# A fused window-attention and two-MLP kernel: w3's product over all eight PSUM banks, and the later pairs' right factors made ahead and kept in DRAM

## The chip, the cores and the metric

The kernel runs on one core of a Trainium2 chip. The metric is device microseconds for one execution. Five engines work side by side, each through its own instructions in their order: PE (matrix products; PEld is its weight load), DVE (VectorE), ACT (ScalarE), POOL (GpSimd) and SP, which here only issues transfers. PE writes its products to PSUM, which has eight banks; the other operands lie in SBUF.

## The reference, cut to what matters

The input is 4 x 576 = 2304 tokens. A causal attention with a window of 128 and a linear bias per head gives x (2304 x 512). Then two MLPs follow:

```python
h = x @ w_in                       # 512 -> 2048
g = s * np.maximum(h, 0.0) ** 2 + b
x2 = g @ w_out                     # 2048 -> 512
a, c = x2 @ w1, x2 @ w2            # 512 -> 1024 each
out = ((a * c) @ w3) @ w_out2      # 1024 -> 1024 -> 512
```

The weights come as 64-bit floats and are turned into 32-bit floats on the chip. The products need more than one pass of PE's fp32r format, so an operand is kept as a high and a low part (hi = the rounded value, lo = value - hi), and each product is three passes: hi·hi, hi·lo, lo·hi.

## The kernel before, in words

Tokens are worked in six tiles of 384. An attention task for a head and a tile runs beside the first MLP of an earlier tile. The changed lines lie in what comes after and around the last tile:

- **The last MLP tile** (`slot`, `mlp_h`, `mlp_relu`, `mlp_g`, `mlp_gl`, `mlp_x`). For each of 16 chunks of d_ff, PE makes `hp` (12 matmuls, L488), ACT and DVE make `gh` and `gl` of it (the high and low part), and PE adds 12 matmuls into the four `acc` banks (L537). The attention is over by then, and each slot offers four places to put other work in. There `w_tick` decodes w1 and w2 chunk by chunk (`w_chunk`: two loads `wr<-w`, an ACT pass, three DVE passes per matrix that join the 64-bit halves, then sums s1 to s4 on DVE, then four splits into hi on ACT and lo on POOL by `split_to`), and `late_load` brings back the prepared pieces of w3 and w_out2.
- **w3's product** (`w3_unit`): w3 @ w_out2 is made once, as w3o, 192 matmuls of 512 columns, in two groups of four PSUM banks; each group is copied out and split (ACT L579, DVE L580) when its eight units are done.
- **The three pairs.** Two token tiles make a pair. x2 @ w1 and x2 @ w2 are taken by blocks with seven products instead of eight (Strassen's scheme): left factors A11 ... S4 come from `w_chunk`, right factors B11, B21, T1, T2, T4, B22, T3 from `x_steps`, each for k = 0, 1, so 14 tiles of a hi and a lo part. `pair_chunk` runs 42 matmuls for each of eight chunks (L736), DVE and POOL combine them into p (DVE L822 for the first tile of the pair, POOL L828 for the second), `p_split` makes ph and pl (ACT L753, DVE L758), and `out_mm` takes p to the output, nine matmuls (L772): for the first tile of the pair inside the loop, one chunk late, for the second tile after the loop (`out_mm(2q+1, c)`, with `out_mm(2q, 7)` among them).
- **Between pairs**: the right factors of pair 0 are made beside w3's product. Those of pairs 1 and 2 are made after the loop of the pair before, beside its last nine `out_mm`: loads of x2 from DRAM (`x2_load`), sums on DVE (L702), the hi parts on ACT (L594), the lo parts on POOL (L595).

Inside these the order on each engine is set by a scheduler that plays the program through a timeline, so what stands in the program is only where work may go. Matmuls of the pairs are kept in program order. SP issues all transfers, in one queue. Tiles of one tag share a few buffers, and a new one waits until an old one is free: `t` (6 buffers: x2 loads and the products' copies m4, m5), `z` (2), `gh` and `gl` (2 each), `w` (33).

Of the kernel before, what the change touches and what calls it, by code (L numbers as in the profile page):

```python
# [18 lines left out]
DM = H * D  # L19
# [16 lines left out]
PASSES = ((0, 0), (0, 1), (1, 0))  # L36


@with_exitstack
def kernel(  # L40
# [481 lines left out]
    def mlp_x(t, c):  # L522
# [5 lines left out]
        for m in range(KD):  # L528
            ms = slice(m * P, (m + 1) * P)
            if t == 0:  # L530
                nc.tensor.matmul(  # L531
                    out=x2acc[m], lhsT=wo[c][:, ms], rhs=g,
                    start=(c == 0), stop=(c == NC1 - 1),
                )
                continue
            for n, (l, r) in enumerate(PASSES):
                nc.tensor.matmul(  # L537
                    out=x2acc[m], lhsT=wo[c][:, l, ms], rhs=g[r],
                    start=(c == 0 and n == 0), stop=(c == NC1 - 1 and n == 2),
                )  # L540
# [25 lines left out]
    def w3_unit(ig, j, accs):  # L566
        if j == 0:
            pool, tag = ((ps_rot, "rot"), (ps_acc, "acc"))[ig]
            accs[:] = [pool.tile([P, DM], F32, tag=tag, name="w3a") for _ in range(4)]
        for i in range(4):  # L570
            for n, (l, r) in enumerate(PASSES):
                nc.tensor.matmul(  # L572
                    out=accs[i], lhsT=w3g[ig, j][:, l, i * P:(i + 1) * P], rhs=wo2s[j][:, r, :],
                    start=(j == 0 and n == 0), stop=(j == NC2 - 1 and n == 2),
                )
        if j == NC2 - 1:
            for i in range(4):
# [18 lines left out]

    def w_chunk(c):
# [48 lines left out]
        tt(out=s3, in0=a11, in1=a21, op=ALU.subtract)  # L646
        yield 1 - c % 2
# [4 lines left out]
        split_to((d[:, 0, dc], d[:, 1, dc]), a22, nc.gpsimd)  # L652
# [3 lines left out]
        for names, src in ((("A11", "A12"), z1), (("S1", "S2"), sv[:, :DM]), (("S3", "S4"), sv[:, DM:])):  # L656
# [5 lines left out]
            split_to((t[:, 0, :], t[:, 1, :]), src, nc.gpsimd)  # L662
# [16 lines left out]
    def x2_load(q, k):  # L679
        for nm, t, m in (  # L680
            ("11", 2 * q, k), ("21", 2 * q, 2 + k), ("12", 2 * q + 1, k), ("22", 2 * q + 1, 2 + k)
        ):
# [64 lines left out]
    def p_split(src):  # L747
        ph = gp.tile([P, TT], F32R, tag="gh", name="ph")
        pl = gp.tile([P, TT], F32R, tag="gl", name="pl")
# [48 lines left out]
    def pair_chunk(q, c):  # L798
# [8 lines left out]
        tt(out=m1, in0=d, in1=m1, op=ALU.add)  # L807
        e = ps_rot.tile([P, TT], F32, tag="rot", name="d5")
# [304 lines left out]
```

## Time and profile before

| | us |
|---|---|
| median of 3 runs (906.1 to 927.08) | 907.81 |
| the profiled execution | 908.04 |
| its span | 906.3 |
| PE busy in the span, 4676 matmuls | 865.2 (95%) |
| PEld, DVE, ACT, POOL busy | 778.3, 578.5, 484.4, 419.8 |

The profile is of one execution. A row of a timeline gives start, duration, engine, line, operation and the tiles (out<-in); in brackets stands the idle time ahead of it and what ended it. Runs of like instructions are merged into one row, and xN is their count. The ends of matmuls are modelled, so PE's pace is read from the starts of rows.

### The profile page before, as it was taken

To read this page: it belongs to the slowest core of one execution; us is meant where nothing else is said; L and a number is where in the kernel's file an instruction comes from. 1 tells how busy PE (TensorE), PEld (TensorE's weight loads), DVE (VectorE), ACT (ScalarE), POOL (GpSimd) and SP (SyncE) were. 2 spreads that over 40 slices of the span, in tenths; PEclk is the share of its full clock that TensorE was granted. 3 is DMA by queue.
4 is the path that set the end of the run, shared out by engine and by line. 5 is a ranking of instruction groups with operands and counts; after the bars stand their busy time and mean duration, and the time that the engine had idled before them with its cause. 6 is when DMAs were issued, how large, how long until landed. Compare 5 with 4: busy or idle time off the path is not lost.

```text
span 906.3 us, 13449 instructions
## 1 busy us (share of the span) xinstructions
PE 865.2 (95%) x4676; PEld 778.3 (86%) x4676; DVE 578.5 (64%) x1146; ACT 484.4 (53%) x1140; POOL 419.8 (46%) x440
## 2 busy tenths in 40 slices
PE   8999898999999999999999899979997999899988
PEld 5766566999999999999999799869995999679986
DVE  5888897767888888788747952493336332553332
ACT  5766657877877777776655553342224222332222
POOL 0157657778667776677545423451116111441110
PEclk8999999999999999999999999989999999999999
DMA  8954522121444454554317576120102000110001
GB/s 312 328 199 148 188 76 88 53 76 54 138 164 167 146 192 149 181 176 159 116 71 273 186 255 238 44 73 1 35 1 70 35 8 28 62 42 1 1 1 71
DMA packets 37076, 104.38 MB, mean 115 GB/s; under 512 B 4368, under 2 KB 10512, under 8 KB 37008
## 3 DMA queue, kind: packets, MB, share of 16 engines
q1 hardware_dynamic: 37008, 103.52, 33.3%
q8 instruction: 37, 0.61, 0.3%
q14 instruction: 31, 0.25, 0.1%
HBM read 82.00 MB, written 21.50 MB: 114 GB/s over the span
## 4 chain that ended last, share of the span: by engine, by line
PE 69%; DVE 13%; issue 7%; ACT 4%; DMA 4%; POOL 2%; SPq 0%; DVEq 0%; POOLq 0%; ACTq 0%
PE acc L537 14%; PE hp L488 13%; PE d L736 10%; PE oacc L772 8%; PE u L736 7%; PE w3a L572 3%; PE pv L418 3%; PE hp L479 2%; PE acc L531 2%; DMA wr<-w 2%; PE s L296 1%; PE s L297 1%; DVE z L629 1%; DVE z L101 1%; DVE x2r L702 1%
## 5 line engine op out<-in xcount | busy, mean ns | idle before, releaser
L488 PE MATMUL hp<-x,w 128*128 128x384 f32 x960 | 186.7, 339 | 2.5 <-DVE pp L378 2.5
L537 PE MATMUL acc<-gh,w 128*128 128x384 f32 x640 | 177.3, 339 | 2.2 <-ACT gh L509 2.2
L488 PEld LDWEIGHTS hp<-x,w 128*128 128x128 f32 x960 | 167.5, 188 | 3.1 <-DVE pp L378 2.6
L828 POOL TENSOR_TENSOR p<-mc 128x384 f32<-128x384 f32 (+2 forms) x30 | 30.8, 1035 | 194.5 <-DVE mc L823 194.5
L537 PEld LDWEIGHTS acc<-gh,w 128*128 128x128 f32 x640 | 115.0, 188 | 3.6 <-ACT gh L509 3.4
L537 PE MATMUL acc<-gl,w 128*128 128x384 f32 x320 | 109.3, 342 | 4.6 <-DVE gl L517 4.5
L736 PE MATMUL d<-xb,wblk 128*128 128x384 f32 x576 | 109.1, 337 | 0.1
L736 PEld LDWEIGHTS d<-xb,wblk 128*128 128x128 f32 x576 | 102.0, 189 | 2.6 <-ACT mc L744 0.6
L346 POOL TENSOR_SCALAR pr<-pr,sm 128x128 f32<-128x128 f32 x120 | 66.1, 565 | 80.7 <-ACT z L144 24.9
L772 PE MATMUL oacc<-w3o,ph 128*128 128x512 f32 x288 | 92.1, 401 | 9.6 <-ACT ph L753 9.6
L736 PE MATMUL u<-xb,wblk 128*128 128x384 f32 x432 | 84.4, 337 | 5.9 <-ACT mc L744 5.9
L381 POOL TENSOR_SCALAR_AFFINE_SELECT pt<-pp 128x768 fp32r<-128x768 f32 x80 | 77.6, 991 | 15.4 <-PE pv L418 6.2
L819 DVE TENSOR_TENSOR mc<-d,mc 128x384 f32<-128x384 f32 x24 | 13.4, 558 | 111.4 <-PE d L736 111.4
L258 POOL TENSOR_TENSOR kb<-qkraw,ka 128x512 fp32r<-128x512 f32 x40 | 56.8, 1420 | 55.1 <-ACT ka L257 54.8
L736 PEld LDWEIGHTS u<-xb,wblk 128*128 128x128 f32 x432 | 76.4, 190 | 6.4 <-ACT mc L744 6.2
L772 PEld LDWEIGHTS oacc<-w3o,ph 128*128 128x128 f32 x288 | 54.2, 191 | 22.2 <-ACT ph L753 11.9
L517 DVE TENSOR_TENSOR gl<-r,gh 128x384 fp32r<-128x384 f32 x80 | 60.5, 757 | 19.9 <-ACT gh L509 18.9
L310 DVE CUSTOM_DVE_ANT_0 ns<-s,relm_sb 128x256 f32<-128x256 f32 (+1 forms) x144 | 52.7, 412 | 28.6 <-PE s L297 20.4
L537 PEld LDWEIGHTS acc<-gl,w 128*128 128x128 f32 x320 | 60.2, 188 | 7.3 <-DVE gl L517 7.1
L595 POOL TENSOR_TENSOR xb<-x2r,xb 128x384 fp32r<-128x384 f32 x42 | 48.1, 1175 | 38.9 <-ACT xb L594 38.9
L499 ACT ACTIVATE r<-hp 128x384 f32<-128x384 f32 x96 | 46.4, 483 | 30.6 <-PE hp L488 23.9
L772 PE MATMUL oacc<-w3o,pl 128*128 128x512 f32 x144 | 59.1, 410 | 3.1 <-DVE pl L758 2.9
(111 smaller groups left out, 1683.4 us busy)
## 6 DMA issues: line engine op xcount, KB each, us to landing
qkraw<-qk SPq DMA_DIRECT2D x41, 448.0 KB, 3.4
late<-st SPq DMA_DIRECT2D x23, 512.0 KB, 3.2
w<-late SPq DMA_DIRECT2D x23, 512.0 KB, 5.3
raw<-w_in SPq DMA_DIRECT2D x16, 512.0 KB, 5.9
raw<-w_out SPq DMA_DIRECT2D x16, 512.0 KB, 6.6
wr<-w SPq DMA_DIRECT2D x16, 512.0 KB, 3.7
st<-w3T SPq DMA_DIRECT2D x15, 512.0 KB, 3.6
vraw<-v SPq DMA_DIRECT2D x20, 256.0 KB, 2.6
```

What stands on the lines that cost most here:

```text
L258: nc.gpsimd.tensor_tensor(out=kl, in0=k_r, in1=k.bitcast(F32), op=ALU.subtract)
L310: nc.vector.tensor_tensor_reduce(out=n[:, i, cs], in0=dst[i][:, cs], in1=relm_sb[:, VARIANT.get(t * NB + i, 0), cs], scale=2.0 ** -(h + 1) ...
L346: nc.gpsimd.tensor_scalar(out=e[:, i, :], in0=e[:, i, :], scalar1=sm[:, i:i + 1], scalar2=1.0, op0=ALU.mult, op1=ALU.mult,)
L381: nc.gpsimd.affine_select(out=o[:, :, :, e, :], in_=pp.bitcast(F32), pattern=[[0, 2], [0, NB], [sign, P]], compare_op=op, fill=0.0, base=0 ...
L488: nc.tensor.matmul(out=hp, lhsT=wi[c][:, l, k * P:(k + 1) * P], rhs=xT[t, k][:, r, :], start=(n == 0), stop=(n == 3 * KD - 1),)
L499: nc.scalar.activation(out=rt[:, :TT], in_=hps.pop((t, c)), func=AF.Relu)
L517: nc.vector.tensor_tensor(out=gl, in0=rt[:, :TT], in1=gh.bitcast(F32), op=ALU.subtract)
L537: nc.tensor.matmul(out=x2acc[m], lhsT=wo[c][:, l, ms], rhs=g[r], start=(c == 0 and n == 0), stop=(c == NC1 - 1 and n == 2),)
L595: eng.tensor_tensor(out=dst[1], in0=src, in1=dst[0].bitcast(F32), op=ALU.subtract)
L736: tc.keep_in_program_order(nc.tensor.matmul(out=dst, lhsT=w[:, l, ks], rhs=xblk[bnm, k][:, r, :], start=(start and n == 0), stop=(n == 5), ...
L772: tc.keep_in_program_order(nc.tensor.matmul(out=oacc[t, i], lhsT=p[l][:, cs], rhs=w3o[c][:, r, :], start=(c == 0 and n == 0), stop=(c == N ...
L828: nc.gpsimd.tensor_tensor(out=x, in0=u2[:, n:n + w], in1=m5[:, n:n + w], op=ALU.mult)
```

## The change

- `w3_unit` takes all eight banks at once and works both groups of a unit together; the copies and splits of all eight w3o tiles stand in `w3_out`, after the product.
- The decode of w1 and w2 is offered two steps at each place of the last tile with a reserve of two buffers; the two loads of a chunk are issued inside the chunk before. Its lo parts go to DVE while the last tile runs and to POOL after it. The late pieces are loaded in the order in which the units need them, ten during the last tile and the rest beside the product.
- `x_later(q + 1)` makes the right factors of the next pair inside the chunks of pair q, a step at four places of a chunk, and stores them to DRAM; `x_fetch` brings all 14 back after the last chunk. `x_steps` is left for pair 0 alone.
- Before the last chunk of a pair, the first two splits of the second tile's p are made, one into the two `z` buffers.
- `mlp_x` makes the two passes with `gh` for all four banks first, and the pass with `gl` after them (save in the last chunk of a tile).

```diff
@@ mlp_x
+        order = [(m, n) for m in range(KD) for n in range(3)]
+        if c < NC1 - 1:
+            order.sort(key=lambda x: x[1] == 2)
+        for m, n in order if t else [(m, 0) for m in range(KD)]:
...
-            for n, (l, r) in enumerate(PASSES):
...
+            l, r = ((0, 0), (1, 0), (0, 1))[n]
...
@@ w3_unit
-    def w3_unit(ig, j, accs):
+    def w3_unit(j, accs):
         if j == 0:
-            pool, tag = ((ps_rot, "rot"), (ps_acc, "acc"))[ig]
-            accs[:] = [pool.tile([P, DM], F32, tag=tag, name="w3a") for _ in range(4)]
-        for i in range(4):
+            accs[:] = [ps_rot.tile([P, DM], F32, tag="rot", name="w3a") for _ in range(4)]
+            accs += [ps_acc.tile([P, DM], F32, tag="acc", name="w3a") for _ in range(4)]
+        for i in range(2 * 4):
...
+    def w3_out(accs):
+        for i in range(2 * 4):
+            z = wp.tile([P, 2, DM], F32R, tag="w", name="w3o")
+            nc.scalar.activation(out=z[:, 0, :], in_=accs[i], func=AF.Copy)
...
@@ w_chunk
+        if c == 0:
+            w_raws(0)
+        raws = wraw.pop(c)
...
         tt(out=s3, in0=a11, in1=a21, op=ALU.subtract)
+        if c + 1 < NC2:
+            w_raws(c + 1)
...
-            split_to((t[:, 0, :], t[:, 1, :]), src, nc.gpsimd)
+            split_to((t[:, 0, :], t[:, 1, :]), src, lo_eng[0])
@@ right factors of the later pairs
+    def x_later(q):
+        def load(nm, k):
+            r = lp.tile([P, TT], F32, tag="t", name="xs", bufs=6)
+            nc.sync.dma_start(out=r, in_=x2_at(q, nm, k))
+            return r
+        def store(nm, k, r):
+            z = zp.tile([P, TT], F32, tag="z", name="xh")
+            split_to((z.bitcast(F32R), r.bitcast(F32R)), r, nc.gpsimd)
+            d = xfd[q, nm, k]
+            nc.sync.dma_start(out=d[:, 0, :], in_=z)
+            nc.sync.dma_start(out=d[:, 1, :], in_=r)
...
+        for k in range(2):
+            for nm in ("11", "21"):
+                a = load(nm, k)
+                yield
+                store("B" + nm, k, a)
+            a, b = load("12", k), load("11", k)
+            yield
+            sub(a, a, b)
+            b = load("22", k)
+            yield
+            sub(b, b, a)
+            store("T1", k, a)
...
+    def x_fetch(q):
+        for nm in FACTORS:
+            for k in range(2):
+                y = x_tile(nm)
+                nc.sync.dma_start(
+                    out=y.rearrange("p a t -> p (a t)").bitcast(F32),
+                    in_=xfd[q, nm, k].rearrange("p a t -> p (a t)"),
+                )
+                xblk[nm, k] = y
@@ the last tile and the product
-        slot(n, n - LEAD, lambda: w_tick(3, max(0, 6 + 2 * NC2 - fresh[0] - 4 * (last + NC1 // 2 - n))))
+        slot(n, n - LEAD, lambda: w_tick(2, 2))
...
+        if n >= last + 3:
+            late_load()
+            late_load()
...
+    lo_eng[0] = nc.gpsimd
...
+    for j in range(NC2):
+        for _ in range(3):
+            if fresh[0] < 3 * NC2:
+                late_load()
+        tick(9 if fresh[0] == 3 * NC2 else 0)
+        w_tick(6, 3 if fresh[0] < 3 * NC2 else 0)
+        w3_unit(j, accs)
+        free_w[0] += 3
+        w_tick(2, 3 if fresh[0] + 2 < 3 * NC2 else 0)
+        next(prep, None)
+    w_tick(99, 8)
...
+    w3_out(accs)
+    w_tick(99)
@@ the pairs
     for q in range(NTILE // 2):
+        more = q + 1 < NTILE // 2
+        prep = x_later(q + 1) if more else iter(())
         for c in range(NC2):
...
-            if more and c == NC2 - 2:
-                x2_load(q + 1, 0)
-            pair_chunk(q, c)
+            if c == NC2 - 1:
+                assert next(prep, None) is None
+                p2 = [p_split(p2_parts(0), spare=True), p_split(p2_parts(1))]
+            pair_chunk(q, c, lambda: next(prep, None))
         if more:
-            x2_load(q + 1, 1)
-            prep = x_steps(q + 1)
-            next(prep)
+            x_fetch(q + 1)
         for c in range(NC2):
-            out_mm(2 * q + 1, c, p_split(p2_parts(c)))
-            if c == 0:
+            out_mm(2 * q + 1, c, p2.pop(0) if p2 else p_split(p2_parts(c)))
+            if c == 1:
                 out_mm(2 * q, NC2 - 1, p1s.pop())
```

How the built order moves is seen at three places. The first is DVE where w3's product ends and pair 0 begins (`wr` and `z` belong to the decode of w1 and w2, `w3a` and `w3o` to w3's product, `mc` to the products of the pair). Before:

```order
L626 TENSOR_SCALAR z<-z 128x512
L629 SCALAR_TENSOR_TENSOR z<-wr,z 128x512
L634 SCALAR_TENSOR_TENSOR z<-wr,z 128x512
L645 TENSOR_TENSOR wr<-z 128x256
L646 TENSOR_TENSOR wr<-z 128x256
L653 TENSOR_TENSOR wr<-wr,z 128x256
L654 TENSOR_TENSOR wr<-z,wr 128x256
L807 TENSOR_TENSOR mc<-d_6877,mc 128x384
L580 TENSOR_TENSOR w3o<-w3a,w3o 128x512 x4
L819 TENSOR_TENSOR mc<-d_6885,mc 128x384
L821 TENSOR_TENSOR mc<-u,mc 128x384
```

The change:

```order
L652 SCALAR_TENSOR_TENSOR z<-wr,z 128x512
L663 TENSOR_TENSOR wr<-z 128x256
L664 TENSOR_TENSOR wr<-z 128x256
L673 TENSOR_TENSOR wr<-wr,z 128x256
L674 TENSOR_TENSOR wr<-z,wr 128x256
L591 TENSOR_TENSOR w3o<-w3a,w3o 128x512 x8
L889 TENSOR_TENSOR mc<-d_6905,mc 128x384
L904 TENSOR_TENSOR mc<-d_6915,mc 128x384
L906 TENSOR_TENSOR mc<-u,mc 128x384
```

Before, the decode of the last chunks stands between the two groups of w3o, ahead of the first sums of pair 0; now the decode's end stands ahead of all eight w3o splits, and pair 0 follows them.

The second place is ACT at the end of pair 0's loop (`ph` is the hi part of p, `xb` a right factor of pair 1, `ov` an output tile). Before:

```order
L744 ACTIVATE mc<-d_7429 128x384
L753 ACTIVATE ph<-mc 128x384
L753 ACTIVATE ph<-p_6931 128x384
L594 ACTIVATE xb<-x2r 128x384 x4
L753 ACTIVATE ph<-p_6931 128x384
L594 ACTIVATE xb<-x2r 128x384
L782 ACTIVATE ov<-oacc 128x512
L753 ACTIVATE ph<-p_6931 128x256
L753 ACTIVATE ph<-p_7081 128x128
L594 ACTIVATE xb<-x2r 128x384
L753 ACTIVATE ph<-p_7081 128x384
L594 ACTIVATE xb<-x2r 128x384 x7
```

The change:

```order
L835 ACTIVATE ph<-mc 128x384
L835 ACTIVATE ph<-p_6977 128x384
L823 ACTIVATE mc<-u 128x384
L823 ACTIVATE mc<-d_7541 128x384
L823 ACTIVATE mc<-u 128x384
L823 ACTIVATE mc<-d_7567 128x384
L835 ACTIVATE ph<-mc 128x384
L835 ACTIVATE ph<-p_6977 128x256
L835 ACTIVATE ph<-p_7166 128x128
L864 ACTIVATE ov<-oacc 128x512
```

Before, the first ph of the second tile follows the last `ph<-mc`, and 13 of the 14 `xb` splits stand among the rest (the last of these rows are left off). Now a ph of the second tile stands ahead of the last chunk's copies, another one (in a `z` buffer) as far ahead as chunk 4, and no `xb` split is left there.

The third place is DVE where chunk 0 of pair 0 hands over to chunk 1. Before:

```order
L822 TENSOR_TENSOR mc<-mc 128x384
L758 TENSOR_TENSOR pl<-mc,ph 128x384
L807 TENSOR_TENSOR mc<-d_6942,mc 128x384
L819 TENSOR_TENSOR mc<-d_6950,mc 128x384
L821 TENSOR_TENSOR mc<-u,mc 128x384
```

The change:

```order
L907 TENSOR_TENSOR mc<-mc 128x384
L732 TENSOR_TENSOR xs<-xs 128x384 x2
L840 TENSOR_TENSOR pl<-mc,ph 128x384
L889 TENSOR_TENSOR mc<-d_6991,mc 128x384
L732 TENSOR_TENSOR xs<-xs 128x384
L904 TENSOR_TENSOR mc<-d_7007,mc 128x384
```

Before, the split `pl<-mc,ph` follows the product `mc<-mc` with nothing between them; now two sums for the next pair's factors (`xs`), each of which needs a load, stand ahead of it, and a third behind it.

## Rows read from the trace of the kernel before

**Rows 1.** Busy time by stretch: us, PE, PEld, DVE, ACT, POOL, granted clock, DMA share, GB/s

```profile
478.00:558.80 80.80, 74.37 (x411) 70.97 (x411) 53.43 (x78) 41.91 (x84) 27.58 (x22) 1.00 0.72 253
558.80:598.70 39.90, 39.90 (x178) 33.03 (x177) 20.78 (x27) 15.36 (x30) 21.79 (x20) 1.00 0.26 84
598.70:707.80 109.10, 97.54 (x481) 87.53 (x480) 54.12 (x85) 36.11 (x78) 35.54 (x31) 0.95 0.08 26
707.80:806.80 99.00, 94.55 (x482) 84.67 (x481) 42.06 (x70) 30.25 (x67) 26.88 (x24) 1.00 0.10 32
806.80:902.20 95.40, 92.66 (x481) 85.09 (x479) 32.76 (x63) 24.59 (x53) 10.29 (x10) 1.00 0.05 17
```

**Rows 2.** PE's waits from 500 us on: us in total, times, longest

```profile
PE oacc L772 <- ACT ph L753: 9.6, 6, 2.7
PE u L736 <- ACT mc L744: 5.9, 1, 5.9
```

**Rows 3.** The chain of waits inside pair 0: start us, us, what

```profile
618.72 2.10 PE oacc L772 x9
...
628.12 2.10 PE oacc L772 x9
```

**Rows 4.** Timeline where pair 0 begins, PE, ACT and DVE

```profile
607.86 2.29 PE L736 MATMUL u<-xb,wblk 128*128 128x384 f32 x6 [5.87 <-ACT mc L744]
...
607.34 0.47 ACT L744 ACTIVATE mc<-u 128x384 f32<-128x384 f32 x1
...
601.88 1.64 DVE L629 SCALAR_TENSOR_TENSOR z<-wr,z 128x512 uint32<-128x512 uint32 x1
...
604.16 0.42 DVE L626 TENSOR_SCALAR z<-z 128x512 uint32<-128x512 uint32 x1
604.62 0.69 DVE L629 SCALAR_TENSOR_TENSOR z<-wr,z 128x512 uint32<-128x512 uint32 x1
```

**Rows 5.** Timeline of PE from the end of pair 0's loop to pair 1

```profile
682.98 0.73 PE L772 MATMUL oacc<-w3o,ph 128*128 128x512 f32 x2 [2.62 <-ACT ph L753]
...
684.29 1.05 PE L772 MATMUL oacc<-w3o,ph 128*128 128x512 f32 x2
...
685.57 1.05 PE L772 MATMUL oacc<-w3o,ph 128*128 128x512 f32 x2
...
707.84 1.23 PE L736 MATMUL u<-xb,wblk 128*128 128x384 f32 x6
```

**Rows 6.** Timeline of one chunk's hand-over in pair 0, DVE, ACT, POOL and PEld

```profile
672.01 0.55 DVE L822 TENSOR_TENSOR mc<-mc 128x384 f32<-128x384 f32 x1
...
672.59 0.53 ACT L753 ACTIVATE ph<-mc 128x384 fp32r<-128x384 f32 x1 [0.20 <-DVE mc L822]
...
673.15 0.70 DVE L758 TENSOR_TENSOR pl<-mc,ph 128x384 fp32r<-128x384 f32 x1 [0.59 <-ACT ph L753]
673.39 1.34 POOL L595 TENSOR_TENSOR xb<-x2r,xb 128x384 fp32r<-128x384 f32 x1
...
675.20 0.19 PEld L772 LDWEIGHTS oacc<-w3o,pl 128*128 128x128 f32 x1
```

**Rows 7.** PE's waits in the last MLP tile, 478 to 560 us

```profile
PE acc L537 <- DVE gl L517: 4.2, 5, 1.5
PE acc L537 <- ACT gh L509: 2.2, 2, 1.6
```

**Rows 8.** Groups of DVE and POOL, 470 to 560 us: busy us, mean ns, idle before

```profile
L629 DVE SCALAR_TENSOR_TENSOR z<-wr,z 128x512 uint32<-128x512 uint32 x10 | 8.0, 798 | 0.3
...
L595 POOL TENSOR_TENSOR wblk<-wr,wblk 128x512 fp32r<-128x512 f32 x7 | 10.5, 1510 | 7.0 <-ACT wblk L594 5.2 <-PE acc L537 1.8
```

**Rows 9.** Transfers: tiles, queue, count, KB each, median us from issue to landing

```profile
w<-late SPq DMA_DIRECT2D x23, 512.0 KB, 5.3
...
x2d<-ev SPq DMA_DIRECT2D x24, 192.0 KB, 3.8
x2r<-x2d SPq DMA_DIRECT2D x24, 192.0 KB, 3.1
```

More of the change, by code (lines that the diff above doesn't have):

```diff
@@ L36 @@
 PASSES = ((0, 0), (0, 1), (1, 0))
+FACTORS = ("B11", "B21", "T1", "T2", "T4", "B22", "T3")
 @with_exitstack
@@ L535, in mlp_x @@
                 continue
-            for n, (l, r) in enumerate(PASSES):
[L537 to L540, printed above, removed]
+            l, r = ((0, 0), (1, 0), (0, 1))[n]
+            nc.tensor.matmul(
+                out=x2acc[m], lhsT=wo[c][:, l, ms], rhs=g[r],
+                start=(c == 0 and n == 0), stop=(c == NC1 - 1 and n == 2),
+            )
         if t == 0:
@@ L676, in w_tick, with x2_at, x_tile, x2_load @@
                 wneed[0] = 0
[L679 to L682, printed above, removed]
+    def x2_at(q, nm, k):
+        return x2d[2 * q + (nm[1] == "2")][k + 2 * (nm[0] == "2")]
+    def x_tile(nm):
+        if nm in ("B11", "B21", "T1"):
+            return lp.tile([P, 2, TT], F32R, tag="xb", name="xb", bufs=6)
+        return xp.tile([P, 2, TT], F32R, tag="x", name="xb")
+    def x2_load(k):
+        for nm in ("11", "21", "12", "22"):
             if k and nm in ("12", "22"):
@@ L745, in keep_copy, with p_split @@
         return y
-    def p_split(src):
-        ph = gp.tile([P, TT], F32R, tag="gh", name="ph")
-        pl = gp.tile([P, TT], F32R, tag="gl", name="pl")
+    def p_split(src, spare=False):
+        if spare:
+            ph, pl = (zp.tile([P, TT], F32R, tag="z", name="pz") for _ in range(2))
+        else:
+            ph = gp.tile([P, TT], F32R, tag="gh", name="ph")
+            pl = gp.tile([P, TT], F32R, tag="gl", name="pl")
         n = 0
@@ L814, in pair_chunk @@
             out_mm(2 * q, c - 1, p1s.pop())
+        step()
         f = ps_rot.tile([P, TT], F32, tag="rot", name="d4")
@@ L817, in pair_chunk @@
         m4 = keep_copy(f, lp, "t")
+        step()
         prod(e, "S4", "B22", c, False)
@@ L831, in pair_chunk @@
             n += w
+        step()
     for c in range(NC1):
@@ L1022 @@
-    assert not todo and not flight
+    for j in range(NC2):
+        for _ in range(3):
+            if fresh[0] < 3 * NC2:
+                late_load()
+        tick(9 if fresh[0] == 3 * NC2 else 0)
+        w_tick(6, 3 if fresh[0] < 3 * NC2 else 0)
+        w3_unit(j, accs)
+        free_w[0] += 3
+        assert free_w[0] >= 0, (j, free_w)
+        w_tick(2, 3 if fresh[0] + 2 < 3 * NC2 else 0)
+        next(prep, None)
+    w_tick(99, 8)
+    free_w[0] -= 8
+    assert free_w[0] >= 0, free_w
```

97 lines of the change are left out of this document (47 added, 50 removed).

## The prediction

> **What bounds the kernel now.** I read the busy times by stretch first [rows 1]. PE is busy for nearly all of every stretch, at the full level of its clock (1.00, 2.4 GHz) but for the one that begins pair 0 (0.95). So PE's work sets the time, and a change that leaves its 4676 matmuls as they are can win only what PE loses between them. The three pairs do the same work and take 109.1, 99.0 and 95.4 us: that is where to look. PE's waits name the culprits [rows 2]: the first hi split of p at the end of a loop (2.7 us at worst), and one wait of 5.9 us for a copy.
>
> What a pair needs at PE's pace comes from the chain of waits [rows 3]. The out_mm of consecutive chunks begin 628.12 - 618.72 = 9.40 us apart, of which out_mm is 2.10 and the 42 matmuls of the products are 7.30. A pair is 7.30 (chunk 0 has no out_mm) + 7 x 9.40 + 9 x 2.10 (behind the loop) = 92.0 us. The three lose 17.1, 7.0 and 3.4, together **27.5 us**.
>
> Three things make up the loss. Where pair 0 begins [rows 4], PE waits 5.87 us for a copy that takes ACT 0.47 us: the copy came only at 607.34, since ACT stood behind splits of the w1/w2 decode, and those behind DVE, on which the decode's steps take 1.64 us where one undisturbed takes 0.69. At the end of a loop [rows 5] PE waits 2.62 us for ph, which stands in ACT's order behind the split of the last chunk's product. After that wait in pair 0 the starts of out_mm's matmuls are 1.28 us apart for three (684.29 to 685.57, so 0.43 each) where the regular pace is 2.10 / 9 = 0.23: the lower level of the clock, 1.2 GHz. And behind the loops of pairs 0 and 1 the splits of p wait among the right factors' splits for ACT and DVE. Pair 2 has no factors to make and loses only 3.4.
>
> **The change, part by part.**
>
> *Start of pair 0.* The decode moves ahead. By the order, seven of eight chunks are decoded on DVE ahead of the last gl, where there were five; before, three were left for w3's product and after it. One chunk and one w3 piece remain for the 39.9 us of the product, in which DVE was busy 20.8 and POOL 21.8 [rows 1]. So the decode should end in time. What is late next is w3_out: eight hi and eight lo splits in a row. But the eight banks finish three matmuls apart, the first 21 matmuls before the end, and pair 0's first banks are those four that come free first. I leave 0.5 us. Bounds: nothing, and the wait that stands there now, 5.87 us.
>
> *Right factors.* The 14 splits and 10 sums of a pair leave the stretch behind the loop and go beside the chunks, where they add 14 ACT splits, 14 POOL splits, 10 sums on DVE, 18 loads, 28 stores, and then 14 fetches on SP's queue. Engine time is there: in the loops PE sets a pace of 9.4 us a chunk, and in all of pair 2, which makes no factors, DVE was busy 32.8 and ACT 24.6 of 95.4 us [rows 1]. The risk is order. In a chunk's hand-over [rows 6] the product mc ends at 672.56, ph at 673.12, pl at 673.85, and PE loads pl at 675.20: **1.35 us of slack**. In the new order two sums stand between mc and pl on DVE, and a sum waits for a load. A load lands 3.1 us after its issue, a store of the same size 3.8 [rows 9], and loads wait for one of six `t` buffers, two of which the chunk's own copies hold. Bounds per pair: nothing, if every load was issued a chunk ahead, or 5 chunks x (3.1 - 1.35) = 8.8 us, if each of the five chunks that carry the factors waits for a whole load. I take 2 us, nearer to nothing: the order spreads the steps over five chunks (47 us), and 18 loads through four buffers, each held for 3.1 + 0.5 + 1.3 + 3.8 = 8.7 us (load, hi, lo, store), need 39 us (hi and lo from [rows 6]). For pairs 0 and 1: 4 us.
>
> The SBUF page of the Trainium skill ("SBUF — State Buffer", section "Who interferes with whom") speaks against this part: a VectorE operation with two SBUF inputs and a GpSimd operation that reads SBUF exclude each other, and the second waits for the whole of the first. The trace agrees for pl, whose inputs mc and ph are both in SBUF: 0.70 us beside POOL work [rows 6]. By this rule each of the 28 POOL splits beside the loops could hold back mc or pl by up to its own duration; what that gives is rival 2.
>
> *Fetch.* 14 tiles of 384 KB are 5.5 MB. The transfers moved 253 GB/s at a busy share of 0.72 in the last tile [rows 1], so 5.5 MB take 22 us at that rate. The first can start when the last chunk has used B11, 8.4 us before the loop ends; the first use is 18.9 us (nine out_mm) after the end, the last 25. So there are 27 us for the first fetches and 33 for all: hidden. Bounds: nothing, and (at a rate half as high) 44 - 33 = 11 us per pair end.
>
> *Splits of the second tile.* With ph and pl for the first two out_mm ready, the waits of 2.6 us and what the clock takes after them go, in all three pairs. The last chunk's own p is then due after two out_mm, 4.2 us after the loop; its pl ends 1.84 us after its mc begins [rows 6], and two sums of mc's kind stand ahead of that, so some 3 us after the last matmul. I leave 0.5 us for each of two pair ends, together 1 us. Bounds: nothing, and the 2.62 us that stand there [rows 5], three times.
>
> *The last MLP tile.* PE waits 4.2 us for gl and 2.2 for gh [rows 7]. With the gl passes last, gl is due four matmuls (0.7 us) later than where the waits stood, which takes up to 0.7 from each of five waits. Against that stands DVE's load. It gets two more chunks of decode, each 2 x (0.42 + 0.69 + 0.69) + 4 x 0.42 = 5.3 us at the undisturbed durations [rows 4] (the four sums of 256 columns put at the 0.42 of the shorter step), and 21 lo splits, at most 0.69 each (the longer step), so 14.5: together 25 us. It is spared POOL's splits beside it: 15 POOL rows of decode (the seven of one form took 1510 ns each [rows 8]) that lengthened a DVE step by about 0.95 (1.64 against 0.69 [rows 4]), 14 us. So DVE goes from 53.4 to about 64.5 busy of 80.8 us: more loaded, not yet the bound. ACT gains 13 hi splits of 512 columns or fewer, at most 0.53 x 512 / 384 = 0.7 us each [rows 6], 9 us on 41.9. I take a gain of 3 us. Bounds: a gain of all 6.4, and a loss of 11, if what DVE gains net stands ahead of gl each time.
>
> *w3's product* is the same 192 matmuls; nothing. Its pieces: in SP's order sixteen loads stand ahead of the last tile's end, as before, which is five of eight units, some 25 of 39.9 us [rows 1]; the other eight need 5.3 us each from issue to landing [rows 9], several at a time.
>
> **Sum**, from the profiled execution's 908.0 us (the median, 907.8, is the same): 908.0 - 27.5 + 0.5 + 4 + 1 - 3 = **883 us**.
>
> **Rivals.**
>
> 1. *The hand-overs come late.* The sums and hi splits of the next pair stand ahead of pl and ph, wait for loads, and PE waits at the out_mm of five chunks in two pairs. For it: the order, the 1.35 us of slack, six shared buffers. Against: 39 us of transfers in 47. At the bound, 2 x 8.8 = 17.5 for the 4 that I took: **897**. Chance 0.13.
> 2. *POOL's splits hold the hand-overs back.* DVE's longer steps at the start of pair 0 (1.64 for 0.69 [rows 4]) run while POOL splits. If two POOL splits meet the mc and the pl of the same hand-over, it is late by 2 x 1.34 - 1.35 = 1.3 us; in half of ten chunks that is 6.5 us: **890**. For it: 28 more POOL rows of 1.34 us beside the loops. Against: pl stood at 0.70 for mc's 0.55 with POOL beside it [rows 6], and POOL's split of 1.34 us meets a given 1.8 us of 9.4 in a third of the cases, two in a row seldom. Chance 0.04. This is what the SBUF page's rule, above, gives here.
> 3. *DVE becomes the bound of the last tile.* For it: 25 us more work, gl behind the decode in one order. Against: the load of 64.5 in 80.8, and gl is due later. The tile loses 11 where I took a gain of 3: **897**. Chance 0.08.
> 4. *The start does not do what it says.* The decode of the last chunk waits for buffers that w3's units hold and still stands in pair 0's way: the 5.87 us and as many matmuls at the low clock as before, some 8 us: **891**. Chance 0.03.
> 5. *Slower than before.* The fetch of 5.5 MB is slow: PE stands at the start of pairs 1 and 2. To lose all 25 us, each pair end must wait 12.5 us, so the fetch must take 33 + 12.5 = 45.5 us, that is less than 121 GB/s. At 84 GB/s, the rate of w3's stretch, it takes 65 us and costs 32 at each of two ends: **947**. Against it: that stretch kept the transfers busy for a share of 0.26 only, so 84 was what was asked for, and 253 / 0.72 and 84 / 0.26 both point to over 320 at a full share. Chance 0.04.
>
> **How the numbers follow.** The forecast has 0.68. Its own range is 874 (all loss gone, and all 6.4 of the last tile) to 893. The range of 8 in 10 takes in its low end and the two rivals at 897, and a little on either side for terms added in round numbers: **872 to 898**. A measurement of this kernel tells about 2% from no change, so faster means under 889.7. That is 0.95 of the forecast, a third of rivals 1 and 3 (which run from there to their bounds) and half of rivals 2 and 4: 0.65 + 0.07 + 0.03 = 0.75. Slower is rival 5, 0.04; within 2% the rest, 0.21.
>
> **What would show it.** In the profile of the changed kernel the three pairs should take 92 to 97 us each, and the granted clock should stay at 1.00 through pair 0. PE's waits after the last tile should hold no wait of 2 us or more; the wait of `u` for `mc` should be gone. If rival 1 holds, PE's waits name ph or pl inside the loops of pairs 0 and 1, ACT's or DVE's waits name `xs` loads, and pair 2 alone is near 92. For rival 2 the rows of mc and pl grow by half a microsecond or more beside POOL. For rival 3 the waits for gl grow in the last tile. For rival 5 PE's first product of pair 1 waits for `xb` from a transfer. The prediction is wrong if pairs 0 and 1 stay above 97 us or the last tile takes longer than 81 us.

## The result and the profile after

The change made the kernel faster: 879.5 us median of four runs (878.3 to 882.4), and a ratio to the kernel before of 0.966, 95% interval [0.957, 0.975]. The ratio is taken over the fast executions of both kernels (906.1, 907.8 and 918.3 us before; one of 927.1 us, in the slow state, is left out). The profiled execution took 882.35 us, 25.7 less than that of before, with a span of 880.6.

The stretches of [rows 1] are now these. The row of the product and those of the pairs begin at PE's first matmul of each, as there. Columns: us, PE, PEld, DVE, ACT, POOL busy, granted clock, DMA share, GB/s.

```profile
478.00:554.30 76.30, 74.70 (x421) 73.03 (x420) 64.34 (x118) 48.62 (x98) 14.41 (x10) 1.00 0.68 232
554.30:594.00 39.70, 39.70 (x177) 32.90 (x176) 16.25 (x22) 14.98 (x28) 20.90 (x18) 1.00 0.54 189
594.00:689.10 95.10, 93.02 (x481) 85.25 (x481) 39.53 (x72) 31.18 (x67) 24.38 (x23) 1.00 0.44 150
689.10:784.40 95.30, 93.14 (x481) 85.16 (x480) 38.09 (x70) 30.59 (x67) 25.45 (x24) 1.00 0.47 164
784.40:876.40 92.00, 92.00 (x480) 85.20 (x480) 32.68 (x62) 24.23 (x53) 10.31 (x10) 1.00 0.05 18
```

The pairs went from 109.1, 99.0 and 95.4 us to 95.1, 95.3 and 92.0: 21.1 us. A tile's last stretch begins at 478 only by choice, so the last tile and the product are better taken together, from the last matmul group of the attention (`pv`) to the first product of pair 0. Before:

```profile
474.46:598.68 124.22, 117.79 (x610) 107.52 (x609) 75.31 (x106) 59.81 (x118) 49.90 (x42) 1.00 0.55 192
```

After:

```profile
476.15:594.04 117.89, 116.29 (x609) 107.79 (x609) 80.70 (x140) 65.18 (x128) 35.31 (x28) 1.00 0.62 214
```

That is 6.3 us. What came earlier ended 1.7 us later (476.15 against 474.46), the end behind the pairs took 4.2 for 4.1: 21.1 + 6.3 - 1.7 - 0.1 = 25.6. The 1.7 hides a larger loss: from the first `pv` group to the last one the kernel before took 403.0 us (71.47 to 474.46) and the changed kernel 406.1 (70.04 to 476.15). The forecast had no term for that.

PE's waits from 470 us on in the changed kernel (total, times, longest), which answer to [rows 2, 7]:

```profile
PE u L815 <- ACT mc L823: 4.0, 4, 1.2
PE acc L546 <- DVE gl L523: 0.8, 1, 0.8
PE acc L546 <- ACT gh L515: 0.7, 1, 0.7
PE oacc L854 <- DVE pl L840: 0.2, 1, 0.2
```

The waits for `ph` (9.6 us in six) and the 5.9 us at the start of pair 0 are gone, and the clock stays at 1.00. Four new waits of about 1 us stand inside the pairs, two each in pairs 0 and 1: PE, about to add the second product into `u`, waits until ACT has copied the first one out (`mc`). The chunks show what they cost. The nine matmuls of out_mm begin at 605.51, 616.15, 625.55, 636.26, 646.03, 655.42 and 665.01, so the chunks take 10.64, 9.40, 10.71, 9.77, 9.39 and 9.59 us where 9.40 is PE's pace: 3.1 us, of which 2.0 is shown as waiting of PE. In the chunks of 9.77 and 9.59 us only the weight load of the second product's matmuls waits for that copy, 0.41 us at 644.87 and 0.24 at 663.86; the rest lies in modelled durations around the two longer waits.

### The profile page after: what moved, and what is told of

It reads as the page before. It is cut to its first block, busy times and chain, and to the rows that moved or that the text cites. A ratio compares the mean times of both kernels' runs of the same rounds, so it can differ in the third digit from the quotient of the medians.

```text
span 880.6 us, 13686 instructions
## 1 busy us (share of the span) xinstructions
PE 857.8 (97%) x4676; PEld 777.2 (88%) x4676; DVE 563.5 (64%) x1167; ACT 485.8 (55%) x1140; POOL 388.6 (44%) x419
## 5 line engine op out<-in xcount | busy, mean ns | idle before, releaser
L546 PE MATMUL acc<-gh,w 128*128 128x384 f32 x640 | 126.3, 339 | 0.8 <-ACT gh L515 0.7
L546 PEld LDWEIGHTS acc<-gh,w 128*128 128x128 f32 x640 | 109.0, 188 | 1.6 <-ACT gh L515 1.4
L352 POOL TENSOR_SCALAR pr<-pr,sm 128x128 f32<-128x128 f32 x120 | 64.5, 552 | 83.0 <-DVE sm L350 22.7
L854 PE MATMUL oacc<-w3o,ph 128*128 128x512 f32 x270 | 84.8, 395 | 0.0
L546 PE MATMUL acc<-gl,w 128*128 128x384 f32 x320 | 69.8, 338 | 2.9 <-DVE gl L523 2.9
L339 ACT ACTIVATE pr<-pr,mn 128x128 f32<-128x128 f32 x120 | 46.9, 392 | 28.0 <-DVE pr L325 27.8
L523 DVE TENSOR_TENSOR gl<-r,gh 128x384 fp32r<-128x384 f32 x80 | 54.2, 678 | 10.4 <-ACT gh L515 9.2
L546 PEld LDWEIGHTS acc<-gl,w 128*128 128x128 f32 x320 | 56.4, 188 | 4.0 <-DVE gl L523 3.9
L854 PEld LDWEIGHTS oacc<-w3o,ph 128*128 128x128 f32 x270 | 50.4, 188 | 10.4
L606 POOL TENSOR_TENSOR xs<-xs,xh 128x384 fp32r<-128x384 f32 x28 | 30.1, 1091 | 64.3 <-ACT xh L605 39.4
```

What stands on the lines that cost most here:

```text
L339: nc.scalar.activation(out=e[:, i, :], in_=e[:, i, :], func=AF.Exp, scale=-1.0, bias=mn[:, i:i + 1], accum_out=sm[:, i:i + 1],)
L352: nc.gpsimd.tensor_scalar(out=e[:, i, :], in0=e[:, i, :], scalar1=sm[:, i:i + 1], scalar2=1.0, op0=ALU.mult, op1=ALU.mult,)
L523: nc.vector.tensor_tensor(out=gl, in0=rt[:, :TT], in1=gh.bitcast(F32), op=ALU.subtract)
L546: nc.tensor.matmul(out=x2acc[m], lhsT=wo[c][:, l, ms], rhs=g[r], start=(c == 0 and n == 0), stop=(c == NC1 - 1 and n == 2),)
L606: eng.tensor_tensor(out=dst[1], in0=src, in1=dst[0].bitcast(F32), op=ALU.subtract)
L854: tc.keep_in_program_order(nc.tensor.matmul(out=oacc[t, i], lhsT=p[l][:, cs], rhs=w3o[c][:, r, :], start=(c == 0 and n == 0), stop=(c == N ...
```

## Experiments

In the tables of pairs below, each pair is again measured from its first product to that of the next, so the startup, which differs from profile to profile, doesn't matter.

**The two halves of the change by themselves.** The first has the changed pairs (`x_later`, `x_fetch`, the early splits) on the start of the kernel before; the second the changed start, with the right factors and the splits behind the loop as before.

```diff
 e_pairsonly: w3_unit, w_chunk, the order of late loads, mlp_x and the last tile's slots as before
 e_startonly:
-                p2 = [p_split(p2_parts(0), spare=True), p_split(p2_parts(1))]
...
+            x2_load(1, q + 1)
+            prep = x_steps()
```

> The pairs of the change (factors made in the loops and fetched, first splits early) behind the w3 product, the decode and the pass order of the kernel before. If the change took PE's lost time away place by place, each place by its own part: pair 0 begins at 598.7 us as before and keeps the stall at its start (some 8.3 us, so 95.1 + 8.3 = 103.4), pairs 1 and 2 take 95.3 and 92.0 as in the changed kernel; the span is 598.7 + 103.4 + 95.3 + 92.0 + 4.2 = 893.6, the time about 895. Rival (the parts hang together: with the decode still running, the next pair's sums and splits collide with it at the start of pair 0): pair 0 takes 107 or more, the time is 899 or more.

> The w3 product, decode and pass order of the change with the pairs of the kernel before. Place by place: pair 0 begins at 594.0, loses the stall at its start (109.1 - 8.3 = 100.8), pairs 1 and 2 stay at 99.0 and 95.4; the span is 594.0 + 100.8 + 99.0 + 95.4 + 4.2 = 893.4, the time about 895, and the two gains (13 and 13) add up to the whole 26. Rival (parts hang together): the sum of the two gains differs from the whole by 4 us or more.

Pairs only: 895.7 us, ratio 0.989 [0.985, 0.993]. Start only: 893.0, ratio 0.985 [0.982, 0.988]. That is 1.07% and 1.50%, each within 0.4; their sum, 2.57%, stands beside the 2.95% (2.68 to 3.22) that the changed kernel gained when it was measured again (below). So the two halves add, as far as these intervals tell. In the pairs-only kernel pair 0 takes 104.8 us and PE waits 6.58 us in it for the copy that stood late before: the start's fault, as in [rows 4]. Pairs 1 and 2 take 95.8 and 92.2.

**The two measures at the end of a loop, taken apart.** One kernel makes the factors behind the loop again and keeps the early splits, one keeps the factors in the loop and drops the early splits.

```diff
 e_nofac:
-            pair_chunk(q, c, lambda: next(prep, None))
+            pair_chunk(q, c, lambda: None)
         if more:
-            x_fetch(q + 1)
+            x2_load(1, q + 1)
+            prep = x_steps()
+            next(prep)
 e_nosplit:
-                p2 = [p_split(p2_parts(0), spare=True), p_split(p2_parts(1))]
```

> The changed kernel with the right factors made behind the loop again; the early splits stay. If early splits cure the 2.6 us wait with the clock's slow matmuls after it (3.4 us, the loss of pair 2 before) and the factors the rest: no waits of about 1 us inside the loops; pair 0 takes 92.0 + (8.7 - 3.4) = 97.3, pair 1 92.0 + (7.0 - 3.4) = 95.6, pair 2 92.0; time about 885. Rival (the factors are the whole loss at the ends of pairs 0 and 1): 100.7 and 99.0, time about 891.

> The changed kernel with the splits of the second tile's p in their old places. If the wait at the loops' ends is the order of ACT alone: 3.4 us more in each pair, 98.5, 98.7 and 95.4, time about 892, PE waits 2.6 us for ph three times. Rival (with the factors out of the way the split is in time anyway): pairs 0 and 1 as in the changed kernel, 882.

They took 889.8 and 892.1 us, in one execution each. Pairs 0 to 2 with the factors behind the loop:

```profile
591.42:690.84 99.42, 94.68 (x481) 85.89 (x480) 44.73 (x72) 31.40 (x68) 26.40 (x24) 0.98 0.08 24
690.84:791.76 100.92, 96.02 (x482) 86.93 (x480) 43.94 (x70) 30.45 (x67) 26.38 (x24) 0.97 0.10 32
791.76:884.00 92.24, 92.24 (x481) 85.25 (x479) 32.70 (x62) 24.45 (x53) 10.30 (x10) 1.00 0.05 18
```

Without the early splits:

```profile
593.19:692.38 99.19, 94.25 (x482) 86.33 (x480) 40.25 (x72) 31.38 (x67) 24.36 (x23) 0.98 0.41 144
692.38:791.22 98.84, 94.36 (x481) 86.44 (x480) 38.16 (x70) 30.74 (x67) 25.42 (x24) 0.98 0.45 158
791.22:886.50 95.28, 92.60 (x481) 85.09 (x479) 32.75 (x62) 24.61 (x53) 10.25 (x10) 1.00 0.05 17
```

With neither (start only) the pairs take 100.8, 98.9 and 95.9. So in these executions either measure alone is worth 1.6 us or less in pairs 0 and 1, or is even a loss, and the two together 5.7 and 3.6. What was expected of e_nofac (97.3 and 95.6 us) did not come; the pairs expected of e_nosplit did, within 0.7 us. The waits tell why. With the factors behind the loop PE's waits for out_mm are these:

```profile
PE oacc L854 <- ACT ph L835: 5.4, 2, 2.7
PE oacc L854 <- DVE pl L840: 4.1, 4, 2.0
```

The two prepared splits only move the wait. In pair 0 PE waits 1.72 us for `pl` in the fifth of the nine out_mm (675.74) and 2.71 us for `ph` in the eighth (684.65), whose splits still stand among the factors' splits; in pair 1 it is the same (1.99 and 2.71 us). With the factors gone and no early split, the first split stands behind the last chunk's, `ph` 8.3 us in three, and the factors' place in the loop has its own price there, 3.8 us in four waits of `u`. Where there are no factors, in pair 2, the early splits alone suffice (92.2).

**The last tile: pass order and the place of the lo parts.** Two parts of the change could have given the 6.3 us.

```diff
 e_noglorder (e_noglorder2 is the same kernel again):
-        order = [(m, n) for m in range(KD) for n in range(3)]
-        if c < NC1 - 1:
-            order.sort(key=lambda x: x[1] == 2)
 e_lopool:
-    wraw, lo_eng = {}, [nc.vector]
+    wraw, lo_eng = {}, [nc.gpsimd]
```

> The changed kernel with the three passes of mlp_x in the old order (gl between the gh passes). The last tile won 4.9 us of PE's waits (6.4 before, 1.5 after). If the order of the passes did it: waits for gl and gh in the last tile of 5 us or more, pair 0 begins at 598 or later. If the decode's move of the lo parts to DVE did it (no POOL beside DVE's steps): waits of 2 to 3 us, pair 0 begins at 595 or 596.

> The changed kernel with the decode's lo parts on POOL in the last tile too. If POOL's splits are what lengthens DVE's steps there (1.64 for 0.69 us) and so makes gl late: DVE's decode steps average 0.8 us or more again, PE's waits for gl in the last tile grow by 3 us or more, pair 0 begins at 597 or later. Rival (DVE's load counts, not its neighbours; 21 splits fewer on DVE): the waits stay at 1.5 or shrink, pair 0 begins at 594 or earlier.

With the old pass order the tile and product lose nothing: 877.8 us in all, 117.4 for the stretch against 117.9. With the lo parts back on POOL the kernel takes 888.3 us, and the stretch is longer than before the change:

```profile
473.61:599.58 125.97, 118.28 (x610) 107.36 (x609) 85.79 (x119) 64.77 (x128) 62.58 (x49) 1.00 0.57 200
```

DVE has 21 instructions fewer in it than in the changed kernel (119 for 140) and is busy 5.1 us longer (85.79 for 80.70). Its groups over 470 to 600 us (busy, mean ns, idle before) show where:

```profile
L647 DVE SCALAR_TENSOR_TENSOR z<-wr,z 128x512 uint32<-128x512 uint32 x16 | 13.9, 870 | 0.4
L644 DVE TENSOR_SCALAR z<-z 128x512 uint32<-128x512 uint32 x16 | 11.3, 709 | 3.2 <-ACT z L636 3.2
```

In the changed kernel, over 470 to 594 us, the same two:

```profile
L647 DVE SCALAR_TENSOR_TENSOR z<-wr,z 128x512 uint32<-128x512 uint32 x16 | 11.0, 689 | 0.3
L644 DVE TENSOR_SCALAR z<-z 128x512 uint32<-128x512 uint32 x16 | 6.8, 424 | 5.1 <-ACT z L636 5.1
```

The same steps last 424 and 689 ns, or 709 and 870 with POOL's splits beside them, and PE's wait for `gl` is 7.1 us in six instead of 0.8 in one (`gl` itself takes 728 ns instead of 634 on average). The rows of e_lopool show the cause one by one:

```profile
525.45 2.57 POOL L606 TENSOR_TENSOR wblk<-wr,wblk 128x512 fp32r<-128x512 f32 x2 [1.36 <-ACT wblk L605]
...
526.77 1.53 DVE L644 TENSOR_SCALAR z<-z 128x512 uint32<-128x512 uint32 x1 [1.26 <-ACT z L636]
```

Of the 32 rows of the two steps nine begin while a split of POOL runs, and eight of these take 0.92 to 1.67 us; the other 23 take 0.42 to 0.43 and 0.68 to 0.69. The ninth (486.83, 0.68 us) stands in a run of DVE steps, and there POOL's split took 4.54 us. Taking the splits off POOL is what gave the tile's gain; the rest of the change to that stretch, without it, loses 1.8 us against the kernel before (125.97 for 124.22).

**The pass order again, measured beside the changed kernel.**

> The changed kernel again, unaltered, on the chip of the next three: about 879 us, pairs 0 and 1 at 95 us each with four waits of u of about 1 us for the copy of m1, and in the four earlier MLP tiles about 2 us of waits of acc for gl. It is the measure for the others.

> The changed kernel with only the pass order of mlp_x put back (gl no longer last). Theory: the new order brings nothing in the last tile (117.4 against 117.9 us in one look) and costs 1.5 to 2 us of gl waits in the four earlier tiles, so 877 to 878 us and a ratio to the changed kernel of 0.998. Rival: the order is what the last tile needs, and the time rises by 2 to 6 us.

The changed kernel took 881.2 us median (878.5 to 882.9), the one with the old order 878.8 (876.6 to 879.0 but for one run of 889.0): 2.4 us less, 0.3%, with intervals of the ratios to before that overlap ([0.968, 0.973] and [0.965, 0.974]), so the times alone do not settle it. The traces do: from the first `pv` group to the last the new order took 406.1, 406.1 and 406.0 us (the changed kernel's two profiles and e_startonly), the old one 403.0, 402.6, 403.9 and 402.8 (before, e_pairsonly, e_noglorder and e_noglorder2). Between 200 and 470 us PE's waits of the changed kernel, in both profiles, are

```profile
PE acc L546 <- DVE gl L523: 2.1, 2, 1.2
```

beside one of 0.2 us for another tile; with the old order, as in the kernel before, there are none. At 222.93 of the second profile PE, which has made its eight `gh` matmuls, waits 1.23 us for `gl`, which stands on DVE behind two attention operations of 1.65 and 1.60 us. With the old order no PE wait is shown in that stretch.

**The fetch, made twice as large.** Each factor is brought from DRAM twice.

```diff
+                for _ in range(2):
                     nc.sync.dma_start(
```

> The changed kernel with each of the 14 factors fetched twice (11 MB at a pair's end). In the changed kernel the 5.5 MB landed between 661.7 and 681 us, 8 us ahead of the first product of pair 1. If bandwidth alone sets it (316 to 408 GB/s in that stretch): 11 MB take 28 to 35 us and end at 690 to 697, the last factor is needed at 695; pair 1 begins 0 to 3 us late, and the time grows by 0 to 5 us. Rival (transfers wait for one another, each second load of a tile for the first): 40 us or more, each of two pair ends waits 6 us or more, time 894 or more.

880.2 us in its one execution, pairs of 95.2 and 95.8 us: 11 MB more to carry, 5.5 at each of two pair ends, show as 0.1 and 0.5 us, and no wait of PE is for a fetched factor. The fetch is hidden with room. In the changed kernel its transfers run at the end of pair 0 so in their busiest 5 us (same columns as the first table; 316 GB/s in the 5 us ahead of it, 392 in those behind):

```profile
670.00:675.00 5.00, 5.00 (x24) 4.11 (x23) 2.26 (x6) 1.07 (x3) 1.27 (x1) 1.00 1.03 408
```

and are over about 8 us before pair 1 begins (689.10).

**The four waits of `u`.** First, an earlier load: two steps of the loop between a load and its use, so that seven chunks carry the factors.

```diff
-            for nm in ("11", "21"):
-                a = load(nm, k)
-                yield
-                store("B" + nm, k, a)
+            a, a2 = load("11", k), load("21", k)
+            yield
+            yield
+            store("B11", k, a)
```

> The changed kernel with two steps instead of one between a factor's load and its use, so that the factors spread over seven chunks instead of five. The four waits of about 1 us in the loops of pairs 0 and 1 come from ACT standing at a hi split (xh) that waits for a DVE sum that waits for a load. If the load's lead is the cause: these waits go, pairs 0 and 1 take 93.0 to 93.5, the time is 878 to 879 in a profile like the changed kernel's 882. Rival (the buffers or POOL, not the lead, hold xh back): waits of 1 us stay, four or more, pairs 0 and 1 at 95 or above.

877.4 us median: still 3.5 us of waits of `u` for `mc`, now in six. The execution profiled took 897 us and lost its time ahead of the pairs, which ran at a granted clock of 1.00 and took 94.6 and 94.8 us (609.70 to 704.33 to 799.09), half a microsecond less than in the changed kernel: not the 93.0 to 93.5 expected if the lead is the cause, and just under the 95 of the rival. In the second of the six the sum `xs` waits for no load:

```profile
646.96 0.55 DVE L911 TENSOR_TENSOR mc<-u,mc 128x384 f32<-128x384 f32 x1
647.43 0.56 DVE L732 TENSOR_TENSOR xs<-xs 128x384 f32<-128x384 f32 x1
647.91 1.38 DVE L910 TENSOR_TENSOR mc<-mc 128x384 f32<-128x384 f32 x1
```

and the product `mc` behind it takes 1.38 us for 0.55. I took POOL's split for the cause, and had it done by DVE. The POOL row beside it is another:

```profile
647.59 1.29 POOL L916 TENSOR_TENSOR p<-mc 128x384 f32<-128x384 f32 x1 [3.33 <-DVE mc L911]
```

```diff
-            split_to((z.bitcast(F32R), r.bitcast(F32R)), r, nc.gpsimd)
+            split_to((z.bitcast(F32R), r.bitcast(F32R)), r, nc.vector)
```

> The changed kernel with the low part of the later pairs' x split computed on DVE, not on POOL. Theory: the POOL split is what makes the four waits of u (beside it mc takes 1.31 us for 0.55, and the stores stand behind it on SP and hold the next loads back): the waits of u go, pairs 0 and 1 take 93 to 93.5 us instead of 95.1 and 95.3, time 875 to 877. Rival: the in-order place of xh, ph and the copy on ACT is the cause whatever makes the low part: the waits stay, and with 14 more DVE operations of about 0.55 us per pair standing before mc and pl the pairs take 95 us or more.

> The two edits together: old pass order of mlp_x and the low part of the later splits on DVE. If both theories hold the gains add: 1.5 to 2 us in the four earlier tiles and 3 to 4 us in pairs 0 and 1, so 873 to 876 us. If only the pass order counts, 877 to 878.

My theory fell: the waits stay and the pairs get longer, as the rival said. DVE splits alone: 885.1 us (881.6 to 893.9). With the old pass order besides (e_best): 881.9, where the old order alone had 878.8 and 873 to 878 was expected. The intervals overlap ([0.970, 0.976] and [0.965, 0.974]), so the profile decides. In e_best PE's waits of `u` rise to

```profile
PE u L812 <- ACT mc L820: 6.4, 6, 2.0
```

and its pairs 0 and 1 take 96.3 and 98.6 us (95.1 and 94.9 in e_noglorder2, with POOL's splits). The longest of the six, on DVE and POOL:

```profile
725.74 0.55 DVE L905 TENSOR_TENSOR mc<-u,mc 128x384 f32<-128x384 f32 x1
726.21 0.55 DVE L603 TENSOR_TENSOR xs<-xs,xh 128x384 fp32r<-128x384 f32 x1
726.67 1.35 DVE L904 TENSOR_TENSOR mc<-mc 128x384 f32<-128x384 f32 x1
...
726.37 1.25 POOL L910 TENSOR_TENSOR p<-mc 128x384 f32<-128x384 f32 x1 [9.70 <-DVE mc L905]
```

No POOL split is near. What stretches `mc` to 1.35 us is POOL's own product of the chunk, `p`, which starts as soon as the second sum (L905) is done. With nothing between, `mc` starts ahead of it, as in pair 2 of the changed kernel:

```profile
811.29 0.55 DVE L908 TENSOR_TENSOR mc<-u,mc 128x384 f32<-128x384 f32 x1
811.76 0.55 DVE L907 TENSOR_TENSOR mc<-mc 128x384 f32<-128x384 f32 x1
...
811.92 0.99 POOL L913 TENSOR_TENSOR p<-mc 128x256 f32<-128x256 f32 x1 [8.14 <-DVE mc L908]
```

Behind `mc` come `ph` and then, in ACT's order, the copy of `u` for which PE waits. In pair 2 that copy and PE's next product into `u` are these two rows, which leave 804.27 - 803.90 = **0.37 us of slack**:

```profile
803.43 0.47 ACT L823 ACTIVATE mc<-u 128x384 f32<-128x384 f32 x1
...
804.27 1.20 PE L815 MATMUL u<-xb,wblk 128*128 128x384 f32 x6
```

Any operation in that chain uses it up, an ACT `xh` ahead of `ph`, or a DVE operation ahead of `mc`, twice so when `mc` then meets POOL. In the changed kernel the first of the four waits reads so:

```profile
612.80 0.75 DVE L732 TENSOR_TENSOR xs<-xs 128x384 f32<-128x384 f32 x1 [0.76 <-DMA xs<-x2d]
613.47 0.54 DVE L907 TENSOR_TENSOR mc<-mc 128x384 f32<-128x384 f32 x1
...
613.63 0.53 ACT L605 ACTIVATE xh<-xs 128x384 fp32r<-128x384 f32 x1 [0.76 <-DVE xs L732]
614.06 0.51 ACT L835 ACTIVATE ph<-mc 128x384 fp32r<-128x384 f32 x1
614.48 0.47 ACT L823 ACTIVATE mc<-u 128x384 f32<-128x384 f32 x1
...
615.00 1.32 PE L815 MATMUL u<-xb,wblk 128*128 128x384 f32 x6 [0.97 <-ACT mc L823]
```

A sum that waited for its load, and an `xh`, stand in the chain. In the other three waits a late sum stands there too:

```profile
631.98 0.56 DVE L732 TENSOR_TENSOR xs<-xs 128x384 f32<-128x384 f32 x1 [1.40 <-DMA xs<-x2d]
...
708.76 0.56 DVE L732 TENSOR_TENSOR xs<-xs 128x384 f32<-128x384 f32 x1 [1.16 <-POOL p L913]
...
727.50 0.56 DVE L732 TENSOR_TENSOR xs<-xs 128x384 f32<-128x384 f32 x1 [1.15 <-DMA xs<-x2d]
```

Two waited for a load; for the third the profile names POOL's `p`, and what held it stays open. So in the changed kernel the late sum makes the waits; with earlier loads (e_spread) the sum is in time, but `mc` then meets POOL's product. That the waits go when every step is kept out of the chain (behind the copy of `u`) wasn't tried.

The fastest version shown beside the changed kernel is the one with the old pass order, by 2.4 us. The earlier loads (877.4) ran on another chip than the changed kernel did either time, so what they gain over it is open, beyond the half microsecond per pair; so is the two together.

## Why the prediction was right, and where it wasn't

The forecast was 883 us, in a range of 872 to 898; the time is 879.5, and 882.35 for the execution profiled. That the sum comes so close is in part luck: against its terms the tile gained 3.3 us more, the pairs lost 0.9 more (6.4 over 3 x 92.0, where 5.5 was left), and 1.8 went in places that had no term. Step by step:

- **PE's pace of 92.0 us a pair** held: pair 2 takes 92.0, with no wait and all 480 matmuls at the full clock.
- **Start of pair 0**: 0.5 us was left, and PE doesn't wait there at all. The decode's last sums end at 587.3, ahead of the first w3o split, as the order had it. They still meet work of POOL (1.40 and 1.51 us for rows whose mean over all eight chunks is 0.66), but now beside w3's product, where nobody waits. The start with the last tile brings 1.50% by itself, the pairs 1.07%.
- **Right factors in the loop**: 2 us a pair was taken, and 2.0 is what PE's waits show, 3.1 and 3.3 what the pairs exceed 92.0 by. So the size was near, if too small; the place was not right. The working priced 1.35 us of slack ahead of out_mm, by `pl` [rows 6], and said that PE's waits would name ph or pl; no wait does, save one of 0.2. The tighter slack was that of the copy of `u`, 0.37 us, on ACT behind the same `ph`. It could have been read where [rows 6] are from: there that copy ends at 673.50 and PE's `u` starts at 673.92, 0.42 us of slack (rows below). "The wait of u for mc should be gone" was wrong in the same way: the one of 5.9 us went, four of 0.8 to 1.2 came.
- **Pair ends**: 1 us was left, and no wait stands there (the one of 0.2 us is in the loop of pair 1, at 701.43). That the early splits and the empty stretch behind the loop work only together was not in the working, which gave the 2.62 us of waits to the early splits and the rest to the factors. e_nofac and e_nosplit, one execution each, show that each alone brings little in pairs 0 and 1.
- **The last MLP tile**: this term was mis-sized and its reason wrong. The working took 3 us, from the pass order (up to 0.7 us for each of five waits) against a DVE that gets busier. Measured are 6.3 with the product, all of it from the lo parts leaving POOL (8.1 us worse with them there), none from the pass order (117.4 us with the old one). The load on DVE came out as worked out (64.3 us busy, 64.5 expected), since the 14 us that POOL's splits had cost DVE were in it; what they meant for `gl` was not. The pass order was priced only in the last tile; it holds for the earlier tiles too, a term that the sum lacks, and costs 2 to 3 us there (406.1 against 402.8 to 403.9 us).
- **Fetch**: hidden, as forecast, and faster than the 253 GB/s taken.

The rows that [rows 6] leave out, of POOL, ACT and PE in the kernel before:

```profile
672.17 1.26 POOL L828 TENSOR_TENSOR p<-mc 128x384 f32<-128x384 f32 x1 [7.99 <-DVE mc L823]
...
673.02 0.48 ACT L744 ACTIVATE mc<-u 128x384 f32<-128x384 f32 x1
...
673.92 1.21 PE L736 MATMUL u<-xb,wblk 128*128 128x384 f32 x6
```

They show a second thing that the working missed. It saw `pl` take 0.70 us "beside POOL work" and thought of POOL's splits. What ran as `pl` began (673.15) was POOL's product `p`, until 673.43, and `pl` ended 0.42 us after that; the split came later, at 673.39.

Of the rivals, the first (late hand-overs) and the second (POOL beside the loops) are both there, but not at their bounds: 3.1 and 3.3 us in the two pairs for both. Of the first rival's signs, DVE's waits do name `xs` loads (13.5 us in nine for pairs 0 and 1). For the second the working said that rows of `mc` and `pl` would grow by half a microsecond or more. In the changed kernel the products `mc` of pairs 0 and 1 mean 572 ns (547 in pair 2, longest 734) and the `pl` behind them 686 (673), so it did not hold there: a split beside `mc` added 0.18 us in two of the four waits (633.38 and 728.91). Where other steps pushed them the products did grow (means of 815 ns in e_spread, 769 in e_best), in the rows shown against POOL's product and not its split. The section "Who interferes with whom" of the Trainium skill's page "SBUF — State Buffer" says that a VectorE operation with two SBUF inputs and a GpSimd operation that reads SBUF exclude each other, the second to issue waiting until the first is done; the trace agrees: `mc` at 726.67 beside a POOL row that runs until 727.62 ends at 728.02, 0.40 us after it. Rivals 3 to 5 did not come: the tile got shorter, the start has no wait, the fetch none.

## What to carry to other kernels

When work is put between the steps of a tight loop, list every chain that leads back to the bounding engine and take the least slack: here it was not the visible hand-over (1.35 us) but a copy two places behind it on another engine (0.37 us). A stall made of two queues (factors and splits behind a loop) yielded to neither cure alone here, so price the pair, not the parts. Before an operation is moved to a less busy engine, see what its neighbours' durations are with and without it: 21 splits given to a less busy POOL cost DVE more time than doing them itself.

## What was not expected of the hardware

- A one-input integer step on DVE (`z<-z`, 128x512) lasts 424 ns on average, and 709 with POOL splits beside it (1.53 us for the row at 526.77, above): not only operations with two inputs from SBUF are held back.
- The length of a wait did not tell what the clock did after it. In e_best it stayed at 1.00 after 1.81 us in pair 0 (first row below); after 1.98 us in pair 1 the row of 731 to 733 us shows 0.50, the 1.2 GHz level, and the matmuls of the next out_mm start 0.43 us apart instead of 0.23 until 733.8. That out_mm takes 3.65 us (730.17 to 733.82) for 2.10, which is most of the 2.3 us by which this pair is longer than pair 0.

```profile
631.70:633.70 2.00, 1.96 (x10) 1.82 (x11) 0.67 (x2) 0.86 (x2) 0.00 (x0) 1.00 0.60 192
...
731.00:733.00 2.00, 2.00 (x6) 1.54 (x5) 1.53 (x3) 0.91 (x2) 0.00 (x0) 0.50 0.01 4
```

  Yet after a wait of 2.21 us in e_fetch2 (PE's `u` at 728.55) the clock stayed at 1.00, and after one of 1.80 us in e_lodve (at 740.82) it was at 0.50:

```profile
730.50:732.50 2.00, 2.00 (x11) 1.72 (x10) 0.56 (x1) 0.44 (x1) 0.39 (x1) 1.00 0.15 55
```

```profile
742.80:744.80 2.00, 2.00 (x6) 1.55 (x5) 1.55 (x3) 1.16 (x3) 0.00 (x0) 0.50 0.00 0
```

- The transfers reached 408 GB/s at a full share, where the busiest stretch of [rows 1] had 253 at 0.72; a store of 192 KB landed 1.9 to 2.2 us after its issue, half of the 3.8 that stood in for it [rows 9].
